# Attention over blocks of 128 keys, one of them shared by two heads, in a fused attention and mixture kernel

## The chip, the cores and the metric

The kernel runs on one NeuronCore of a Trainium2 chip. The metric is the device time of one execution in microseconds (us); the time of a kernel is the median of several executions. The engines are TensorE (PE; its weight loads are listed apart as PEld), VectorE (DVE), ScalarE (ACT), GpSimd (POOL) and SyncE (SP, which here only issues transfers).

## The reference

```python
# 2 batches, 12 heads, 448 rows, head width 64; float32
scores = cap * tanh((q @ k.T / 8) / cap)
attn = exp(scores - rowmax);  attn /= attn.sum(-1) + 1e-9
x = (attn @ v)                      # -> 896 tokens x 768
h = x @ w_in;  x = relu(h)**2 @ w_out          # 768 -> 2048 -> 768, weights float64
e = argmax over 8 experts of cosine(x, emb) / tau
out = gate * relu(x @ w1[e]) @ w2[e]           # 768 -> 1024 -> 768, per token
```

## The kernel before

All matrix work is in float32 of one of two kinds. "f32r" operands go through TensorE in one pass; a product is made exact enough by splitting an operand into a high part (a cast to f32r) and the low rest, and adding two or three products. Plain f32 products go through TensorE as two instructions per matmul, each with a weight load of its own. The array keeps one operand in place (the weights, loaded by LDWEIGHTS) and streams the other one, one column after the other.

The program is written out in order for each engine; each engine takes its own instructions strictly in that order and waits on semaphores. `attention()` is a generator over the 24 heads; the first 13 heads run alone (stage one), and when it yields "batch" the rest is interleaved with the first dense layer, `mlp(0)` (stage two). Then come `mlp(1)`, the routers and the experts, which the change leaves alone but for the order of rows in a chunk of the output.

For each head of the kernel before:

- `load_head` brings q and twice k with rows on 112 partitions (one DMA of q, two of k), `load_v` brings v. A DMA waits until the eighth one before it has landed.
- `split_q` (on POOL) casts q to its high part and subtracts it for the low one. `front_k` (L338) turns k on TensorE, four f32 transposes into PSUM tile `kp`; `front_q` (L352) turns the two parts of q, four f32r transposes into `qp`. VectorE (ScalarE in stage two) casts `kp` to `kh` (L341, L343), VectorE subtracts for the rest `kl` (L345), and `qp` is copied to `q2` (L355, L357).
- `scores` has four blocks of 112 keys, and for each one two f32r matmuls with 448 columns (L371, L372), a tanh by ScalarE (L373) and, for two blocks together, an exp (L374). The result `p_t` stands with keys on partitions.
- `values` multiplies with v: weights are 64 columns of v and 64 of ones, `p_t` is streamed with 448 columns, in plain f32, so 8 passes per head (L384). The ones give the sums of the softmax in 64 rows.
- ScalarE copies the sums into `den` (L393), and `finish` inverts 128x448 of them for two heads (L412) and multiplies (L415); then follow the high part `xh` (L409) and the rest `xl` (L410).

During stage one VectorE also narrows the first dense weights from float64 to float32 (`convert_early`, four operations per chunk, L186 to L189 and L281).

Of the kernel before, what the change touches and what calls it, by code (L numbers as in the profile page):

```python
# [20 lines left out]
def kernel(  # L21
# [22 lines left out]

    nc = tc.nc
# [13 lines left out]
    T = 64  # L59
    OOB = 4096.0  # L60
# [20 lines left out]
    vt = [ap.tile([CP, NC, 2, D], F32, tag=f"vt{i}", name=f"vt{i}", bufs=1) for i in range(2)]  # L81

    def load_head():
        n = nload[0]
        if n >= len(order):
            return
        nload[0] = n + 1
        b, h = order[n]
        q_r = ap.tile([CP, NC, D], F32, tag="q_r", name=f"q_r{n}", bufs=2)
        k_r = ap.tile([CP, NC, 2, D], F32, tag="k_r", name=f"k_r{n}", bufs=2)  # L90
        kk = k[b, h].rearrange("(p c) d -> p c d", c=NC)
        qq = q[b, h].rearrange("(p c) d -> p c d", c=NC)
        e = nc.sync if n else nc.scalar
        if n < 2:
            nc.sync.dma_start(q_r, qq)
        e.dma_start(k_r[:, :, 0, :], kk)
        nc.sync.dma_start(k_r[:, :, 1, :], kk)
        if n >= 2:
            nc.sync.dma_start(q_r, qq)
        raw[n] = (q_r, k_r)  # L100

    def load_v(n):
        b, h = order[n]
        nc.sync.dma_start(vt[n % 2][:, :, h % 2, :], v[b, h].rearrange("(p c) d -> p c d", c=NC))
# [10 lines left out]
    NWARM = 7  # L115
# [4 lines left out]
    def warm(n):  # L120
        for _ in range(n):
            nc.tensor.matmul(idle[:, :S], zero[:, :P], zero, start=True, stop=True)

    warm(NWARM)
    ident = const.tile([P, P], F32, name="ident")
    make_identity(nc, ident)
    identr = const.tile([P, P], F32R, name="identr")
    nc.vector.tensor_copy(identr, ident)
    for i in range(2):
        nc.gpsimd.memset(vt[i][:, :, 1 - i, :], 1.0)  # L130
# [18 lines left out]
    ATN, R1N = 78, 40  # L149
    WC, WM = 4, 3  # L150
    DRIP = 1
    PS, PB = 48, 6
# [116 lines left out]
    def convert_early(step):  # L269

        i, odd = divmod(step, 2)
        if not odd:
            if 0 < i <= len(early):
                c = early[i - 1]
                nc.sync.dma_start(c["keep"](), c["f"])
            if i + 1 < len(early):
                raw_w(early[i + 1], 1001 + i)
        elif i < len(early):
# [3 lines left out]
            for step in narrow(c):  # L282
                step()
# [39 lines left out]
    def attention():  # L323
        pair = {}

        def split_q(n):
            q_r = raw[n][0]
            q_s = ap.tile([CP, NC, 2, D], F32R, tag="q_s", name=f"q_s{n}", bufs=2)
            e = nc.gpsimd if n else nc.vector
            e.tensor_copy(q_s[:, :, 0, :], q_r)  # L330
            e.tensor_tensor(q_s[:, :, 1, :], q_r, f32(q_s[:, :, 0, :]), op=ALU.subtract)
            st[n] = [q_s]

        def front_k(n):
            k_r = raw.pop(n)[1]
            kp = ps.tile([P, S], F32, tag="tr", name=f"kp{n}", bufs=2)
            for c in range(NC):
                nc.tensor.transpose(kp[:, c * CP:(c + 1) * CP], k_r[:, c].rearrange("p t d -> p (t d)"), ident[:CP, :CP])  # L338
            kh = ap.tile([P, S], F32R, tag="kh", name=f"kh{n}", bufs=2)
            if eng["kh"] == "dve" and n:  # L340
                nc.vector.tensor_copy(kh, kp)  # L341
            else:
                nc.scalar.copy(kh, kp)  # L343
            kl = ap.tile([P, S], F32R, tag="kl", name=f"kl{n}", bufs=2)
            nc.vector.tensor_tensor(kl, kp, f32(kh), op=ALU.subtract)  # L345
            st[n] += [kh, kl, []]

        def front_q(n):
            q_s = st[n][0]
            qp = ps.tile([P, S], F32R, tag="tr", name=f"qp{n}", bufs=2)  # L350
            for c in range(NC):
                nc.tensor.transpose(qp[:, c * CP:(c + 1) * CP], q_s[:, c].rearrange("p t d -> p (t d)"), identr[:CP, :CP])  # L352
            q2 = ap.tile([P, S], F32R, tag="q2", name=f"q2{n}", bufs=2)
            if eng["kh"] == "dve":
                nc.vector.tensor_copy(q2, qp)  # L355
            else:
                nc.scalar.copy(q2, qp)  # L357
            st[n][0] = q2

        def front(n):  # L360
            split_q(n)
            load_head()
            front_k(n)

        def scores(n, hf):
            q2, kh, kl, pl = st[n]
            p_t = ap.tile([CP, 2, S], F32, tag="p_t", name=f"p_t{n}_{hf}", bufs=4)
            for j in range(2):
                c = 2 * hf + j
                sc = bank("sc", f"sc{n}_{c}")  # L370
                nc.tensor.matmul(sc[:CP, :S], kh[:, c * CP:(c + 1) * CP], q2, start=True, stop=False)  # L371
# [5 lines left out]
        def values(n):  # L377
# [5 lines left out]
            for c in range(NC):  # L383
                nc.tensor.matmul(pv[:, :S], vv[:, c], pl[c // 2][:, c % 2], start=c == 0, stop=c == NC - 1)  # L384
                if c == 1:
                    yield
# [726 lines left out]
```

## Time and profile before

| | |
|---|---|
| median of 3 runs | 535.78 us (534.64 to 536.04) |
| the profiled execution | 535.34 us, its span from first to last instruction 533.6 us |
| PE busy, granted clock | 98%, 0.995 |
| DVE, ACT, POOL busy | 72%, 58%, 7% |
| stage one, stage two | from about 13 to 82 us, from 82 to about 260 us |

How to read it: busy time is the time in which an engine has at least one instruction in hand. Matmuls overlap in the pipeline, so the duration of one says less than the distance from its start to the next one's start.

### The profile page before, as it was taken

To read this page: it belongs to the slowest core of one execution; us is meant where nothing else is said; L and a number is where in the kernel's file an instruction comes from. 1 tells how busy PE (TensorE), PEld (TensorE's weight loads), DVE (VectorE), ACT (ScalarE), POOL (GpSimd) and SP (SyncE) were. 2 spreads that over 40 slices of the span, in tenths; PEclk is the share of its full clock that TensorE was granted. 3 is DMA by queue.
4 is the path that set the end of the run, shared out by engine and by line. 5 is a ranking of instruction groups with operands and counts; after the bars stand their busy time and mean duration, and the time that the engine had idled before them with its cause. 6 is when DMAs were issued, how large, how long until landed. Compare 5 with 4: busy or idle time off the path is not lost.

```text
span 533.6 us, 7630 instructions
## 1 busy us (share of the span) xinstructions
PE 521.8 (98%) x2558; PEld 439.9 (82%) x2558; DVE 386.7 (72%) x667; ACT 308.3 (58%) x563; POOL 36.4 (7%) x67
## 2 busy tenths in 40 slices
PE   8999999999999999999999999999999999999994
PEld 6676667888888888879999899999889898998993
DVE  4799999999979897989398666645448444556751
ACT  5999899788877878875344331322453233444530
POOL 2221212011011100001000000000000000000000
PEclk9999999999999999999999999999999999999997
DMA  6876994778655858584724213345612245645641
GB/s 145 220 200 154 233 248 136 216 240 270 193 177 184 258 172 249 177 273 155 245 89 135 81 41 118 107 143 155 173 40 80 84 135 170 198 150 153 216 135 38
DMA packets 110713, 87.88 MB, mean 165 GB/s; under 512 B 37442, under 2 KB 97346, under 8 KB 110672
## 3 DMA queue, kind: packets, MB, share of 16 engines
q1 hardware_dynamic: 101904, 81.92, 51.8%
q10 hardware_dynamic: 8672, 5.42, 3.7%
q8 instruction: 21, 0.34, 0.3%
q14 instruction: 20, 0.16, 0.1%
q0 software_dynamic: 96, 0.04, 0.0%
HBM read 69.43 MB, written 18.28 MB: 164 GB/s over the span
## 4 chain that ended last, share of the span: by engine, by line
PE 91%; DVE 4%; ACT 2%; issue 0%; DVEq 0%; ACTq 0%
PE pv L384 11%; PE h L482 7%; PE y L482 7%; PE y L483 7%; PE h L484 7%; PE h L483 7%; PE y L484 7%; PE z L482 4%; PE e L482 4%; PE e L483 4%; PE z L484 4%; PE z L483 4%; PE e L484 4%; PE sc L371 3%; PE sc L372 3%; PE kp L338 1%
## 5 line engine op out<-in xcount | busy, mean ns | idle before, releaser
L215 DVE TENSOR_TENSOR wl<-wf,wh 128x512 fp32r<-128x512 f32 (+1 forms) x140 | 110.3, 799 | 52.5 <-ACT wh L209 50.9
L209 ACT CAST wh<-wf 128x512 fp32r<-128x512 f32 (+1 forms) x97 | 65.8, 697 | 24.4 <-DVE orow L909 8.8
L384 PE MATMUL pv<-p_t,vt 112*128 112x448 f32 x192 | 78.1, 540 | 0.8 <-DVE den L415 0.8
L482 PE MATMUL h<-xh,wh 128*128 128x448 f32 x192 | 76.0, 396 | 0.0
L482 PE MATMUL y<-gh,wh 128*128 128x448 f32 x192 | 75.1, 391 | 0.0
L483 PE MATMUL y<-gh,wl 128*128 128x448 f32 x192 | 70.2, 366 | 0.0
L484 PE MATMUL h<-xl,wh 128*128 128x448 f32 x192 | 70.2, 366 | 0.0
L483 PE MATMUL h<-xh,wl 128*128 128x448 f32 x192 | 70.2, 365 | 0.0
L484 PE MATMUL y<-gl,wh 128*128 128x448 f32 x192 | 70.1, 365 | 0.0
L373 ACT ACTIVATE p_t<-sc,rcap 112x448 f32<-112x448 f32 x96 | 55.4, 629 | 6.6 <-PE sc L372 6.4
L384 PEld LDWEIGHTS pv<-p_t,vt 112*128 112x128 f32 x192 | 36.1, 189 | 25.5 <-issue 22.8
L374 ACT ACTIVATE p_t<-p_t,capb 112x896 f32<-112x896 f32 x48 | 50.1, 1044 | 1.6
L512 ACT ACTIVATE r<-h 128x448 f32<-128x448 f32 x32 | 17.3, 541 | 40.3 <-PE h L484 25.4
L482 PEld LDWEIGHTS h<-xh,wh 128*128 128x128 f32 x192 | 36.1, 188 | 5.2 <-issue 2.4
L483 PEld LDWEIGHTS h<-xh,wl 128*128 128x128 f32 x192 | 36.2, 188 | 4.8 <-issue 2.4
L482 PEld LDWEIGHTS y<-gh,wh 128*128 128x128 f32 x192 | 36.1, 188 | 4.5 <-issue 1.9
L483 PEld LDWEIGHTS y<-gh,wl 128*128 128x128 f32 x192 | 36.2, 188 | 4.3 <-issue 1.9
L484 PEld LDWEIGHTS h<-xl,wh 128*128 128x128 f32 x192 | 36.1, 188 | 3.2 <-DVE xl L410 0.2
L484 PEld LDWEIGHTS y<-gl,wh 128*128 128x128 f32 x192 | 36.1, 188 | 2.9
L371 PE MATMUL sc<-q,kh 128*112 128x448 f32 x96 | 37.3, 389 | 1.1 <-ACT p_t L373 0.9
L211 DVE CAST wh<-wf 128x512 fp32r<-128x512 f32 (+1 forms) x43 | 20.7, 481 | 23.4 <-PE y L484 19.3
L482 PE MATMUL z<-hh,wh 128*128 128x448 f32 x96 | 36.4, 379 | 0.0
(232 smaller groups left out, 942.2 us busy)
## 6 DMA issues: line engine op xcount, KB each, us to landing
wr<-in_moe_w_in_dram SPq DMA_DIRECT2D x16, 768.0 KB, 5.9
wr<-in_moe_w_out_dram SPq DMA_DIRECT2D x24, 512.0 KB, 4.7
wf<-in_moe_w_dram SPq DMA_DIRECT2D x24, 384.0 KB, 3.4
wf<-in_moe_w_dram SPq DMA_DIRECT2D x36, 256.0 KB, 3.2
wf<-wk SPq DMA_DIRECT2D x20, 384.0 KB, 4.0
wk<-wf SPq DMA_DIRECT2D x16, 384.0 KB, 2.8
wk<-wf SPq DMA_DIRECT2D x24, 256.0 KB, 2.7
wf<-wk SPq DMA_DIRECT2D x24, 256.0 KB, 2.9
```

The source lines that it names most:

```text
L209: nc.scalar.copy(c["hi"], c["f"])
L211: nc.vector.tensor_copy(c["hi"], c["f"])
L215: nc.vector.tensor_tensor(c["lo"], c["f"], f32(c["hi"]), op=ALU.subtract)
L371: nc.tensor.matmul(sc[:CP, :S], kh[:, c * CP:(c + 1) * CP], q2, start=True, stop=False)
L372: nc.tensor.matmul(sc[:CP, :S], kl[:, c * CP:(c + 1) * CP], q2, start=False, stop=True)
L373: nc.scalar.activation(p_t[:, j], sc[:CP, :S], AF.Tanh, scale=rcap[:CP])
L374: nc.scalar.activation(p_t, p_t, AF.Exp, scale=capb[:CP])
L384: nc.tensor.matmul(pv[:, :S], vv[:, c], pl[c // 2][:, c % 2], start=c == 0, stop=c == NC - 1)
L482: nc.tensor.matmul(o, wh, xh, start=first, stop=False)
L483: nc.tensor.matmul(o, wl, xh, start=False, stop=False)
L484: nc.tensor.matmul(o, wh, xl, start=False, stop=last)
L512: nc.scalar.activation(r, o[:, :S], AF.Relu)
```

## The change

The two heads of a pair hold 2 x 448 = 896 keys, which are now cut in seven blocks of 128: three of the first head, one in which 64 keys of each head stand, and three of the second. The blocks of all pairs form one stream, taken in groups of two.

- q and k come with 32 x 32 squares on partitions (four DMAs per head, runs of 32 numbers), v as 128-row blocks of 64 columns and one column of ones (two DMAs per head). VectorE turns the squares in one STREAM_TRANSPOSE of 128x448 (`turn`); TensorE turns neither q nor k.
- The keys' high and low parts stand on the two halves of the partitions of one tile `kp`; `qh` holds q's high part twice, `ql` zeros and q's low part. A block's scores are two matmuls as before, four for the shared block, whose keys of the other head are zero columns in `kp`.
- In `split_k` and `split_q` the casts are VectorE's (ScalarE's in stage two), the subtraction for k VectorE's, the second copy and the subtraction for q POOL's. All of them read and write SBUF.
- `values` takes `p_t` as the weights (112 columns at a time) and streams v and the ones: 65 columns, 130 in the shared block. The sums are now a column of the product, so `divide` inverts 112x8 numbers. `finish` turns the rows of a pair back with four f32 transposes on TensorE.
- The products of a pair gather in two PSUM banks. Stage one has two such pairs of banks, stage two one.
- The narrowing of the first weights is handed out one operation per group, and 12 matmuls on zeros stand at the start, where 8 stood.

```diff
-        q_r = ap.tile([CP, NC, D], F32, tag="q_r", name=f"q_r{n}", bufs=2)
-        k_r = ap.tile([CP, NC, 2, D], F32, tag="k_r", name=f"k_r{n}", bufs=2)
+        qk = ap.tile([P, S // SQ, SQ], F32, tag="qk", name=f"qk{n}", bufs=3)
+        for i, a in enumerate((k, q)):
+            halves = a[b, h].rearrange("(s t) (j d) -> j t s d", t=SQ, d=SQ)
+            for j in range(2):
+                e = nc.scalar if n == 0 and j else nc.sync
+                o = (2 * (1 - i) + j) * SQ
+                e.dma_start(qk[o:o + SQ], halves[j])
...
+        def turn(n):
+            qk = raw.pop(n)
+            load_head()
+            tq = ap.tile([P, S], F32, tag="tq", name=f"tq{n}", bufs=2)
+            nc.vector.transpose(tq, qk.rearrange("p s d -> p (s d)"))
+            kp = ap.tile([P, S + D], F32R, tag="kp", name=f"kp{n}", bufs=3)
+            i = n % 2
+            nc.gpsimd.memset(f32(kp[:, :D] if i else kp[:, S:]), 0.0)
+            qh = ap.tile([P, S], F32R, tag="qh", name=f"qh{n}", bufs=3)
...
+        def split_k(n):
+            tq, keys, _, _ = front[n]
+            copy(keys[D:], tq[D:])
+            nc.vector.tensor_tensor(keys[:D], tq[D:], f32(keys[D:]), op=ALU.subtract)
...
+            copy(qh[:D], tq[:D])
+            (nc.gpsimd if n > 1 else nc.vector).tensor_copy(qh[D:], tq[:D])
+            nc.gpsimd.tensor_tensor(ql[D:], tq[:D], f32(qh[:D]), op=ALU.subtract)
...
+        KINDS = [(0, c) for c in range(KB)] + [None] + [(1, c) for c in range(KB)]
...
+                for t, c in parts:
+                    h = st[2 * m + t]
+                    for x in (1, 2):
+                        nc.tensor.matmul(sc[:, :S], h[0][:, c * P:(c + 1) * P], h[x],
...
+                for t in range(NC):
+                    o = acc_[m][t // 2][:, t % 2]
+                    w = p_t[:, j, t * CP:(t + 1) * CP]
...
+                    nc.tensor.matmul(o, w, x, start=i == 0 and t % 2 == 0, stop=i == NK - 1, skip_group_check=True)
+                if i == NK - 1:
+                    divide(m)
+                    if j == 0:
+                        yield from wait(2)
...
+        for g in range(G):
+            if g + 2 < G:
+                scores(g + 2)
                 yield
+                yield from fronts(g + 2)
+            yield from values(g)
```

On PE in stage one, one head of the program before reads as follows. `kp` and `qp` are the turned k and q, `sc` the scores, `pv` the product with v; "x2" counts matmuls, each of which is two passes where operands are plain f32.

```order
L338 MATMUL kp_317<-ident,k_r_203 128x112 x4
L371 MATMUL sc_0_327<-q_285,kh_266 112x448
L372 MATMUL sc_0_327<-q_285,kl_268 112x448
L371 MATMUL sc_1_331<-q_285,kh_266 112x448
L372 MATMUL sc_1_331<-q_285,kl_268 112x448
L352 MATMUL qp_336<-identr,q_s_309 128x112 x4
L371 MATMUL sc_2_344<-q_285,kh_266 112x448
L372 MATMUL sc_2_344<-q_285,kl_268 112x448
L371 MATMUL sc_3_348<-q_285,kh_266 112x448
L372 MATMUL sc_3_348<-q_285,kl_268 112x448
L384 MATMUL pv_361<-p_t_0_270,vt_81 128x448 x2
L384 MATMUL pv_361<-p_t_1_287,vt_81 128x448 x2
```

On PE in the same stage, a group of the changed program and the next one: a shared block (`sc_3`, four matmuls with the keys of two heads), a whole block, and the products of an earlier group; `xp` is a pair's rows turned back.

```order
L400 MATMUL sc_3_314<-qh_206,kp_204 128x448
L400 MATMUL sc_3_314<-ql_121,kp_204 128x448
L400 MATMUL sc_3_314<-qh_241,kp_239 128x448
L400 MATMUL sc_3_314<-ql_119,kp_239 128x448
L400 MATMUL sc_4_320<-qh_241,kp_239 128x448
L400 MATMUL sc_4_320<-ql_119,kp_239 128x448
L421 MATMUL pv_0_244<-vt_82,p_t_254 112x65 x2
L421 MATMUL pv_1_245<-vt_82,p_t_254 112x65 x2
L421 MATMUL pv_0_336<-vt_83,p_t_254 112x65 x2
L421 MATMUL pv_1_337<-vt_83,p_t_254 112x65 x2
...
L458 MATMUL xp_380<-ident,rows_329 128x112 x4
```

The eight transposes of a head are gone, four stand behind every second head, and four matmuls of 448 columns became sixteen matmuls of 65 or 130 columns per group.

On DVE in stage one, what stands for two heads before (`kh`, `kl`, `q` from PSUM, the reciprocal of `den` and two products):

```order
L341 CAST kh_322<-kp_317 128x448
L345 TENSOR_TENSOR kl_324<-kp_317,kh_322 128x448
L355 COPY q_341<-qp_336 128x448
L412 RECIPROCAL den_251<-den_251 128x448
L415 TENSOR_TENSOR den_251<-pv_245,den_251 64x448
L415 TENSOR_TENSOR den_251<-pv_302,den_251 64x448
L341 CAST kh_382<-kp_377 128x448
L345 TENSOR_TENSOR kl_384<-kp_377,kh_382 128x448
L355 COPY q_401<-qp_396 128x448
L410 TENSOR_TENSOR xl_357<-den_251,xh_356 128x448
```

On DVE in the changed program, from the division of a pair to the fifth head's parts; L195 and L197 narrow weights:

```order
L438 TENSOR_SCALAR rs_330<-pv_0_244,ecap 112x4
L438 TENSOR_SCALAR rs_330<-pv_1_245,ecap 112x4
L439 RECIPROCAL rs_330<-rs_330 112x8
L442 TENSOR_TENSOR rows_329<-pv_0_244,rs_330 112x256
L442 TENSOR_TENSOR rows_329<-pv_1_245,rs_330 112x256
L195 SCALAR_TENSOR_TENSOR wf_275<-wr_216,wf_275 128x768
L347 STREAM_TRANSPOSE tq_358<-qk_232 128x448
L380 CAST kp_360<-tq_358 64x448
L359 TENSOR_TENSOR kp_360<-tq_358,kp_360 64x448
L380 CAST qh_362<-tq_358 64x448
L197 SCALAR_TENSOR_TENSOR wf_275<-wr_216,wf_275 128x768
```

The reciprocal shrank from 128x448 to 112x8 numbers, and a head's three operations from PSUM became four from SBUF, of which POOL's copy and subtraction of 64x448 use the results.

## Rows read from the trace of the kernel before

**Rows 1.** The chain of work that ended last, shares of the span by engine.
```profile
PE 91%; DVE 4%; ACT 2%; issue 0%; DVEq 0%; ACTq 0%
```
**Rows 2.** Two windows: us, busy (count) of PE PEld DVE ACT POOL, clock, DMA, GB/s.
```profile
16.00:82.00 66.00, 64.76 (x288) 42.62 (x287) 62.03 (x77) 61.80 (x91) 15.31 (x24) 1.00 0.81 204
82.00:260.00 178.00, 178.00 (x846) 148.38 (x846) 160.28 (x230) 140.08 (x256) 14.46 (x27) 1.00 0.69 212
```
**Rows 3.** Timeline of PE in stage one: start us, us, engine, line, operation, tiles, count.
```profile
66.93 0.45 PE L352 MATMUL qp<-identr,q_s 112*128 112x112 f32 x4
...
67.48 0.36 PE L372 MATMUL sc<-q,kl 128*112 128x448 f32 x1
...
68.08 3.17 PE L384 MATMUL pv<-p_t,vt 112*128 112x448 f32 x8
71.09 0.55 PE L338 MATMUL kp<-ident,k_r 112*128 112x112 f32 x4
...
71.68 0.36 PE L372 MATMUL sc<-q,kl 128*112 128x448 f32 x1
```
**Rows 4.** Timeline of PE's weight loads in stage one.
```profile
66.02 0.18 PEld L371 LDWEIGHTS sc<-q,kh 128*112 128x112 f32 x1
66.12 0.18 PEld L372 LDWEIGHTS sc<-q,kl 128*112 128x112 f32 x1
```
**Rows 5.** Timeline of PE and its loads around a small f32 matmul (cum, two passes).
```profile
406.22 0.32 PE L719 MATMUL cum<-noh,su 112*112 112x64 f32 x2
...
406.32 0.19 PEld L482 LDWEIGHTS e<-x2h,wh 128*128 128x128 f32 x1
...
406.44 0.19 PEld L483 LDWEIGHTS e<-x2h,wl 128*128 128x128 f32 x1
406.64 0.36 PE L483 MATMUL e<-x2h,wl 128*128 128x448 f32 x1
```
**Rows 6.** Groups of instructions in stage one: busy us, mean ns of one, idle before.
```profile
L373 ACT ACTIVATE p_t<-sc,rcap 112x448 f32<-112x448 f32 x48 | 27.7, 627 | 1.4 <-PE sc L372 1.1
L374 ACT ACTIVATE p_t<-p_t,capb 112x896 f32<-112x896 f32 x25 | 26.1, 1043 | 0.8
...
L412 DVE RECIPROCAL den<-den 128x448 f32<-128x448 f32 x6 | 17.6, 2942 | 0.0
...
L345 DVE TENSOR_TENSOR kl<-kp,kh 128x448 fp32r<-128x448 f32 x12 | 7.5, 624 | 0.4
L341 DVE CAST kh<-kp 128x448 fp32r<-128x448 f32 x12 | 7.5, 621 | 4.2 <-PE kp L338 4.0
...
L415 DVE TENSOR_TENSOR den<-pv,den 64x448 f32<-64x448 f32 x10 | 6.2, 622 | 0.3
```
**Rows 7.** Instructions of POOL's lines L330 and L331: ns min/median/max.
```profile
L330 POOL CAST q_s<-q_r x23: 397/398/1202, 5.2 to 180.0; 112x256 fp32r<-112x256 f32 x23
L331 POOL TENSOR_TENSOR q_s<-q_r,q_s x23: 726/737/1328, 5.7 to 180.5; 112x256 fp32r<-112x256 f32 x23
```
**Rows 8.** Instructions of VectorE's cast from SBUF to SBUF.
```profile
L500 DVE CAST gh<-r x32: 383/386/589, 93.4 to 322.2; 128x448 fp32r<-128x448 f32 x32
```
**Rows 9.** Timeline of DVE and POOL where they meet in stage two.
```profile
88.07 0.40 POOL L330 CAST q_s<-q_r 112x256 fp32r<-112x256 f32 x1 [4.81 <-PE qp L352]
...
88.09 0.62 DVE L345 TENSOR_TENSOR kl<-kp,kh 128x448 fp32r<-128x448 f32 x1
...
88.56 0.74 POOL L331 TENSOR_TENSOR q_s<-q_r,q_s 112x256 fp32r<-112x256 f32 x1
88.63 1.48 DVE L215 TENSOR_TENSOR wl<-wf,wh 128x768 fp32r<-128x768 f32 x1
```
**Rows 10.** Timeline of DVE in stage two, two operations in a row.
```profile
112.10 0.62 DVE L410 TENSOR_TENSOR xl<-den,xh 128x448 fp32r<-128x448 f32 x1
112.64 0.38 DVE L500 CAST gh<-r 128x448 fp32r<-128x448 f32 x1
```
**Rows 11.** Timeline of PE at the start, its last wait before the stream.
```profile
12.55 0.46 PE L371 MATMUL sc<-q,kh 128*112 128x448 f32 x1 [0.40 <-ACT p_t L373]
```

More of the change, by code (lines that the diff above doesn't have):

```diff
@@ L267, with convert_early, first @@
     early = []
[L269 to L278, printed above, removed]
+    def convert_early():
+        def first(i):
             c = early[i]
@@ L348, in front_q @@
[L348 to L371, printed above, removed]
-                nc.tensor.matmul(sc[:CP, :S], kl[:, c * CP:(c + 1) * CP], q2, start=False, stop=True)
-                nc.scalar.activation(p_t[:, j], sc[:CP, :S], AF.Tanh, scale=rcap[:CP])
-            nc.scalar.activation(p_t, p_t, AF.Exp, scale=capb[:CP])
-            pl.append(p_t)
@@ L377, in values @@
[L377 to L393 removed]
+        rows = {}
@@ new lines, in divide @@
+        def divide(m):
+            rows[m] = ap.tile([CP, NC, 2, D], F32, tag="rows", name=f"rows{m}", bufs=1)
+            rs = ap.tile([CP, NC, 2], F32, tag="rs", name=f"rs{m}", bufs=2)
+            pv = acc_.pop(m)
+            for t in range(2):
+                nc.vector.tensor_scalar(rs[:, 2 * t:2 * t + 2], pv[t][:, :, :, D], ecap[:CP], None, op0=ALU.add)
+            nc.vector.reciprocal(rs, rs)
+            for t in range(2):
+                c = slice(2 * t, 2 * t + 2)
+                nc.vector.tensor_tensor(rows[m][:, c], pv[t][:, :, :, :D],
+                                        rs[:, c].unsqueeze(3).to_broadcast([CP, 2, 2, D]), op=ALU.mult)
@@ L395, in finish @@
         def finish(m):
             b, h = order[2 * m]
-            den = pair.pop(("d", m))
+            r = rows.pop(m)
             if h == 0:
@@ L422, in attention @@
-        N = len(order)
-        todo = []
-        split_q(0)
-        front_q(0)
-        front_k(0)
-        warm(1)
-        load_head()
+            tp = ps.tile([P, S], F32, tag="tr", name=f"xp{m}", bufs=2)
+            for c in range(NC):
+                nc.tensor.transpose(tp[:, c * CP:(c + 1) * CP], r[:, c].rearrange("p t d -> p (t d)"), ident[:CP, :CP])
+            nc.scalar.copy(xh[:, cc], tp)
+            late.append(lambda: nc.vector.tensor_tensor(xl[:, cc], tp, f32(xh[:, cc]), op=ALU.subtract))
@@ new lines, in fronts, with run_all @@
+        def fronts(g):
+            for m, i in blocks[2 * g:2 * g + 2]:
+                if i in (1, 2, 5, 6):
+                    n = 2 * m + 2 + (i > 4)
+                    if n < N:
+                        if i in (1, 5):
+                            turn(n)
+                            split_k(n)
+                        else:
+                            split_q(n)
+                        yield
+        def run_all(l):
+            while l:
+                l.pop(0)()
+        todo, late, front = [], [], {}
@@ L471, in attention @@
             yield
-        split_pair()
+        run_all(late)
     for n in range(2):
```

208 lines of the change are left out of this document (104 added, 104 removed).

## The prediction

> **What bounds the kernel now.** I read the chain of waits first: 91% of the span lies on TensorE [rows 1]. The windows then tell stage by stage how near the others are. In stage one (16 to 82 us) PE is busy for 64.8 of 66 us, but VectorE for 62.0 and ScalarE for 61.8 as well; in stage two PE is busy throughout, VectorE for 160 of 178 [rows 2]. So a saving on PE counts in full, as long as VectorE and ScalarE give back at least as much. The granted clock is 1.00 in both.
>
> Busy time cannot price a matmul, so I take distances between starts [rows 3]. Three score matmuls from 67.48 to 68.08 make 0.20 us each. The 8 passes of the product with v take 68.08 to 71.09, 3.01, or 0.376 a pass. The four turnings of k begin at 71.09; the second score matmul behind them starts at 71.68, the first one's 0.20 before that, so they take 0.39. In the same way the four of q take 67.28 - 66.93 = 0.35. A pair of heads costs PE 16 x 0.20 + 2 x (3.01 + 0.39 + 0.35) = 10.7 us.
>
> **The change on TensorE.** Removed, for 24 heads: 24 x 3.01 = 72.2 for the products, 9.4 and 8.4 for turning k and q, together 90.0. The scores stay: seven blocks, one of them with four matmuls, are 16 matmuls of 448 columns per pair, as 2 x 8 were. Added: the product takes `p_t` as weights, so each pass has a weight load of 112 columns and streams 65 columns. Per pair there are 6 x 4 x 2 = 48 such passes and 8 with 130 columns, 576 and 96 in all.
>
> What does one cost? Streaming 65 columns is 65/448 of 0.376, or 0.055; 130 columns are 0.11. A load of 112 columns follows the one before it after 0.10 (66.02 to 66.12) [rows 4]. Whether the two overlap is the main question, and one place shows it: cum, f32 in two passes, 112 weight columns, 64 streamed. Its first pass starts at 406.22; the next line's weights begin at 406.32 and the ones after that at 406.44, and L483 starts at 406.64, so the 0.20 of the matmul in front of it began at 406.44 [rows 5]. Two passes and the load of 128 columns that follows take 0.22: about 0.10 for the first pass and 0.11 or 0.12 for the second. That is the loads alone; streaming is hidden under them. I take 0.10 and 0.11: 576 x 0.10 + 96 x 0.11 = 68.2. The turned rows `xp` are four f32 transposes per pair, 12 x 0.39 = 4.7. Added 72.9, removed 90.0: **-17.1 us**. The bounds: 0.055 a pass if only streaming counted (-43), 0.155 if nothing overlapped (+24, a rival below).
>
> A rule speaks against this. The Trainium skill (TensorE: Matmul & The Clock Gate, Part 3, The mechanism) says that LDWEIGHTS overlaps matmuls in flight only when the row group differs, and all these weights span the same rows. By it nothing would overlap; the trace does not agree, since serial passes would have moved the 406.44 start by another 0.05.
>
> **VectorE and POOL in stage one.** A pair costs PE 16 x 0.20 + 48 x 0.10 + 8 x 0.11 + 0.39 = 9.3 us, so both must fit there. Before, VectorE had 62.0/6 = 10.3 per pair [rows 2]. The reciprocal (2.94), two products (1.24) and six operations from PSUM (6 x 0.62) of that go [rows 6]; about 2.4 are left, for `xl` and the narrowing. New per head are the square transpose, two casts and a subtraction. The casts are SBUF to SBUF, 0.39 [rows 8], the subtraction 0.62 as L345. The transpose is in no row: between the cast's 0.39 and the reciprocal's 2.94 for the same 128x448; I take 0.62, the price of everything else that handles one number per lane and step, and keep 2.94 as a rival. That makes 2 x 2.02. `divide` is two products of half the columns (at most 1.24) and three tiny operations; I take 1.5. Together 2.4 + 4.0 + 1.5 = 7.9, less some 0.08 for each of 17 operations, since 112.10 to 112.64 is 0.54 for one listed with 0.62 [rows 10]: about 6.6. ScalarE's seven blocks need 7 x 0.63 + 3.5 x 1.04 = 8.1 and a copy [rows 6]. Both fit under 9.3.
>
> The trouble is where the operands lie. POOL's copy and subtraction grow from 256 to 448 columns: 0.40 to 0.70 and 0.74 to 1.29 if scaled [rows 7], together 1.1 to 2.0 per head. And where POOL meets VectorE the row at 88.63 shows a subtraction of two SBUF operands stretched from 0.95 to 1.48 by a POOL operation of 0.74 begun 0.07 earlier, while L345, with an operand in PSUM, kept its 0.62 beside POOL's cast [rows 9]. Before, q and k were handled from PSUM; now from SBUF. At that rate (0.5 of 0.74) POOL's 4.0 per pair may cost VectorE up to 2.8: 6.6 + 2.8 = 9.4, just at PE's 9.3.
>
> The Trainium skill (SBUF — State Buffer, Who interferes with whom) says the same more strictly: VectorE in a two-port mode or with two SBUF inputs and GpSimd share a port pair, and the later one blocks fully. By it the meeting would cost all 4.0 a pair; the row shows about two thirds.
>
> So what runs late is the chain to q's low part, and it is shortest in slack for the second head of every other pair (blocks 5 and 6 in one group). Count from the start of those scores. PE still does 0.8 for them, then 1.6 of products, 0.39 of `xp`, 0.8 of scores, 1.7 of products and 0.8 of the next scores before it needs it: 6.1. VectorE enters `divide` 0.8 earlier and leaves at 0.7; one narrowing step (0.95) to 1.7, transpose to 2.3, cast, subtraction and cast to 3.7, POOL's subtraction to 5.0, with POOL's copy (0.70) in between 5.7, and one block by a narrowing step (0.5) 6.2. That is even with PE. I charge 0.4 us per pair for the six pairs of stage one, **+2.4**; 0 if it always fits. In stage two PE has dense layers in between, and the casts are ScalarE's; VectorE loses 3 us of work per pair and gains contention, and I charge nothing. The next pair's accumulators there wait for `divide`, with at least 3 us of other matmuls ahead of them (15 of 0.20): covered unless VectorE is 1.5 late, then up to 1 us for each of five pairs.
>
> **The start.** Before, PE streams from 12.55 on [rows 11], with 14 scores and three heads' turnings done (2.8 + 2.2): 7.5 lost. After, VectorE must turn and split three heads one after the other (some 2.2 each with its waits), then POOL subtracts (1.3), before the eighth block; from a first landing near 4 us that is 12.0 to 12.7, with 14 scores, 16 passes and a block (4.8) done: 7.9 lost, **+0.4**, give or take 1.5. The six DMAs per head replace four; each waits for the eighth before it, and two heads' lead (9 us) covers that. The DMA share is 0.81 in stage one [rows 2], so this cover is not large.
>
> **Sum.** Span 533.6 - 17.1 + 2.4 + 0.4 = 519.3; the profiled run had 1.7 around its span, and the median of the runs stands 0.4 above it: 521.4. I say **521.5 us**, 2.7% faster.
>
> **Rivals.**
> - *No stall and cheaper passes.* The chain always fits and a pass is 0.09: another 2.4 + 6 less, 513. For it: 6.6 of 9.3 is not much for VectorE. Against: the load distance of 0.10.
> - *VectorE and POOL take turns in stage one.* If POOL's 4.0 fully add to VectorE's unshortened 7.9, a pair takes 11.9 against 9.3: 6 x 2.6 = 15.6 in place of 2.4, 535, no change. Half of it gives 527. For it: 88.63; against: `divide` and `xl` read PSUM, and POOL can work beside them.
> - *Loads do not hide (slower).* A pass costs 0.10 + 0.055, one of 130 columns 0.21: 576 x 0.155 + 96 x 0.21 = 109.4 in place of 68.2, 563. It decides at a mean of (90.0 - 4.7)/672 = 0.127 per pass. Against it: rows 5, but they are one place with two passes, not a run of 16.
> - *The transpose is slow (slower).* At 2.94, VectorE has 4.6 more per pair: 11.2 before any contention, 12 to 14 with it, so +3 to 5 in each of six pairs, and in stage two 25 more on 160 of 178: 540 to 555.
>
> **How the numbers follow.** Forecast (516 to 527) 0.60; no stall 0.11; half of the port (527 to 534) 0.14; all of it, no change 0.05; loads not hidden 0.04; slow transpose or a starved queue 0.06. No change means within 0.3%, 1.6 us, about what a measurement of this kernel can tell. Faster 0.85, same 0.05, slower 0.10. The range 514 to 531 leaves about 0.2 out.
>
> **What would show it.** A run of 16 product passes in 1.6 us, with loads 0.10 apart; the square transpose near 0.62; VectorE's casts and subtractions stretched where POOL is at work, and score matmuls of the second head of every other pair waiting for POOL's `ql`; stage two starting near 73 instead of 82. Wrong would be passes above 0.127, PE waiting more than 1 us per pair, a lower granted clock in stage one, or PE idle at the division in stage two.

## The result, and the profile after

The changed kernel takes 531.24 us, median of 4 runs (530.42 to 532.13), beside 535.91 for the kernel before: ratio 0.9915, 95% interval 0.989 to 0.9941. It is faster by 4.7 us, where 14 were predicted; 531.24 lies just above the range's 531. Its profiled execution has a span of 529.4 us. Twelve later runs of the same program have a median of 533.93 (ratio 0.9959), so the gain is about 2 to 5 us.

The windows of the changed kernel, stage one from 16 us on, stage two, and the stretch of [rows 2], columns as there:

```profile
16.00:74.00 58.00, 55.47 (x454) 52.95 (x453) 53.80 (x103) 49.99 (x70) 28.15 (x36) 1.00 0.89 207
74.00:241.00 167.00, 158.01 (x950) 145.46 (x949) 141.17 (x235) 119.39 (x218) 19.01 (x26) 1.00 0.71 206
82.00:260.00 178.00, 169.01 (x998) 155.60 (x997) 142.92 (x239) 121.02 (x227) 19.12 (x34) 1.00 0.71 212
```

Stage one ends at 74 us, not 82, as foretold. But from 82 to 260 us, where TensorE was busy for 178.0 of 178 us, it now stands idle for 9.0, although VectorE and ScalarE have less to do there than before (142.9 and 121.0 us).

Multiplying each stretch's matmuls by the distance between their starts gives TensorE's work; what is left of the stretch is idle. Matmuls on zeros at the start do not count as work:

| stretch (ends before / after, us) | work before | after | idle before | after |
|---|---|---|---|---|
| to the first product with v (13.1 / 12.3) | 5.4 | 2.8 | 7.7 | 9.5 |
| to the first dense matmul (82.2 / 73.8) | 67.2 | 56.5 | 1.9 | 5.0 |
| to attention's last work (237.1 / 240.4) | 152.8 | 153.7 | 2.0 | 12.9 |
| to the end (533.6 / 529.4) | 282.8 | 276.6 | 13.8 | 12.3 |

Work fell by 18.6 us; idle rose by 1.9 + 3.1 + 10.9 and fell by 1.5 at the end, 14.4 in all; -18.6 + 14.4 = -4.2, the spans' difference. The entries depend on the distances taken: with the median distance of each kind of matmul in each profile, work falls by 17.4 and idle changes by +2.2, +2.3, +10.9 and -2.3. Either way most of the loss lies in stage two.

TensorE's waits of the changed kernel, first in stage one (13 to 74 us), then in stage two (74 to 241): what waited for what, us in total, times, longest. Stage two of before has no row in this view.

```profile
PE pv L421 <- DMA vs<-in_v_dram: 1.7, 2, 1.4
PE sc L400 <- POOL kp L350: 0.9, 1, 0.9
PE pv L421 <- DMA vt<-in_v_dram: 0.8, 1, 0.8
...
PE pv L421 <- issue: 3.7, 2, 2.5
PE xp L458 <- DVE rows L442: 2.1, 1, 2.1
PE h L525 <- ACT r L555: 1.8, 2, 1.6
PE x2t L568 <- ACT xf L589: 1.3, 2, 0.9
```

"issue" is a name without a cause. The timeline of TensorE and VectorE shows it; TensorE's last dense matmul started at 97.66 us:

```profile
100.57 0.68 PE L421 MATMUL pv<-vt,p_t 128*112 128x65 f32 x5 [2.55 <-issue]
...
97.12 0.95 DVE L223 TENSOR_TENSOR wl<-wf,wh 128x768 fp32r<-128x768 f32 x1
98.00 0.39 DVE L543 CAST gh<-r 128x448 fp32r<-128x448 f32 x1
98.42 0.63 DVE L544 TENSOR_TENSOR gl<-r,gh 128x448 fp32r<-128x448 f32 x1
98.96 0.55 DVE L194 TENSOR_SCALAR wf<-wf 128x768 int32<-128x768 int32 x1
...
100.04 0.75 DVE L442 TENSOR_TENSOR rows<-pv,rs 112x256 f32<-112x256 f32 x2
```

The product is the next pair's first one. It starts when VectorE has read the old pair's first bank out of PSUM (the first of the two operations of L442), and that read stands behind work on weights and on the dense layer. From 91.87 us on VectorE works without a pause, and GpSimd meets it there once:

```profile
92.37 1.47 POOL L366 TENSOR_TENSOR ql<-tq,qh 64x448 fp32r<-64x448 f32 x1 [2.66 <-PE sc L400]
...
92.81 1.28 DVE L543 CAST gh<-r 128x448 fp32r<-128x448 f32 x1
```

That cast takes 0.39 when alone (98.00 above), so in this row GpSimd accounts directly for 0.9 of the 2.55 us; from 94.2 us to the pause's end it does nothing. A second chain ends at ScalarE; its waits in stage two, and the rows around 136 us:

```profile
ACT kp L382 <- DVE tq L347: 21.3, 8, 5.8
...
135.52 0.96 DVE L197 SCALAR_TENSOR_TENSOR wf<-wr,wf 128x768 int32<-128x768 int32 x1
136.40 0.64 DVE L347 STREAM_TRANSPOSE tq<-qk 128x448 f32<-128x448 f32 x1
...
137.07 0.56 ACT L382 CAST kp<-tq 64x448 fp32r<-64x448 f32 x1 [5.85 <-DVE tq L347]
137.65 0.55 ACT L555 ACTIVATE r<-h 128x448 f32<-128x448 f32 x1
```

ScalarE reached k's cast 5.85 us before the transpose that it needs. The relu L555 stood behind the cast, and TensorE behind the relu (1.8 us). Before, this cast waited for TensorE's own turning, 2.3 us in three times.

### The profile page after: what moved, and what is told of

It reads as the page before. It is cut to its first block, busy times and chain, and to the rows that moved or that the text cites. A ratio compares the mean times of both kernels' runs of the same rounds, so it can differ in the third digit from the quotient of the medians.

```text
span 529.4 us, 8393 instructions
## 1 busy us (share of the span) xinstructions
PE 507.0 (96%) x2898; PEld 461.8 (87%) x2898; DVE 372.7 (70%) x715; ACT 282.2 (53%) x521; POOL 58.1 (11%) x100
## 4 chain that ended last, share of the span: by engine, by line
PE 70%; DVE 12%; DMA 6%; issue 5%; ACT 3%; SPq 2%; POOL 0%; ACTq 0%; DVEq 0%; POOLq 0%
PE y L525 6%; PE y L526 6%; PE y L527 6%; PE pv L421 6%; PE h L525 5%; PE h L527 5%; PE h L526 5%; PE z L525 4%; PE e L525 4%; PE e L526 4%; PE e L527 4%; PE z L527 4%; PE z L526 4%; PE sc L400 4%; DVE wl L223 3%
## 5 line engine op out<-in xcount | busy, mean ns | idle before, releaser
L223 DVE TENSOR_TENSOR wl<-wf,wh 128x512 fp32r<-128x512 f32 (+1 forms) x140 | 112.4, 814 | 63.4 <-ACT wh L217 58.7
L525 PE MATMUL h<-xh,wh 128*128 128x448 f32 x192 | 72.0, 375 | 1.8 <-ACT r L555 1.8
L525 PE MATMUL y<-gh,wh 128*128 128x448 f32 x192 | 72.3, 376 | 0.0
L421 PEld LDWEIGHTS pv<-vt,p_t 128*112 128x112 f32 x576 | 62.8, 178 | 7.4 <-issue 4.8
L421 PE MATMUL pv<-vt,p_t 128*112 128x65 f32 x576 | 62.3, 259 | 4.5 <-issue 3.7
L402 ACT ACTIVATE p_t<-sc,rcap 128x448 f32<-128x448 f32 x84 | 49.0, 630 | 16.9 <-PE sc L400 16.9
L403 ACT ACTIVATE p_t<-p_t,capb 128x896 f32<-128x896 f32 x42 | 43.9, 1044 | 1.4
L400 PE MATMUL sc<-qh,kp 128*128 128x448 f32 x96 | 37.4, 389 | 3.0 <-DVE kp L359 1.8
L366 POOL TENSOR_TENSOR ql<-tq,qh 64x448 fp32r<-64x448 f32 x23 | 30.8, 1339 | 61.0 <-ACT qh L382 33.1
L555 ACT ACTIVATE r<-h 128x448 f32<-128x448 f32 x32 | 17.2, 538 | 37.8 <-PE h L527 25.7
```

Source lines behind the costliest of these rows:

```text
L223: nc.vector.tensor_tensor(c["lo"], c["f"], f32(c["hi"]), op=ALU.subtract)
L366: nc.gpsimd.tensor_tensor(ql[D:], tq[:D], f32(qh[:D]), op=ALU.subtract)
L400: nc.tensor.matmul(sc[:, :S], h[0][:, c * P:(c + 1) * P], h[x], start=t == parts[0][0] and x == 1, stop=t == parts[-1][0] and x == 2)
L402: nc.scalar.activation(p_t[:, j], sc[:, :S], AF.Tanh, scale=rcap)
L403: nc.scalar.activation(p_t, p_t, AF.Exp, scale=capb)
L421: nc.tensor.matmul(o, w, x, start=i == 0 and t % 2 == 0, stop=i == NK - 1, skip_group_check=True)
```

## The experiments

All times are medians of 4 to 12 runs, each beside runs of the kernel before (535.5 to 536.0 us).

| kernel | us | ratio to before (95%) |
|---|---|---|
| changed kernel again | 533.93 | 0.9959 (0.9938 to 0.998) |
| wait4 | 528.53 | 0.9848 (0.9824 to 0.9872) |
| late_k | 530.60 | 0.9913 (0.9885 to 0.9941) |
| wait4_late_k | 525.47 | 0.9802 (0.9783 to 0.9821) |
| pool_out | 530.59 | 0.9903 (0.9881 to 0.9926) |
| v_early | 535.35 | 0.9983 (0.9968 to 0.9998) |
| v_early_fill | 535.60 | 0.9999 (0.9981 to 1.0017) |
| wr_actq | 547.61 | 1.0217 (1.0194 to 1.0241) |
| wlk_v4 | 524.58 | 0.9812 (0.9781 to 0.9842) |
| wlk_qk_long | 523.02 | 0.9778 (0.9755 to 0.9801) |
| wlk_ps44 | 531.62 | 0.9937 (0.9906 to 0.9968) |
| wlk_ps56 | 530.80 | 0.9910 (0.9894 to 0.9926) |
| wlk_v4_pool | 527.60 | 0.9841 (0.9817 to 0.9865) |
| wlk_v4_start | 525.08 | 0.9807 (0.9785 to 0.983) |
| wlk_v4_split2 | 524.95 | 0.9785 (0.9759 to 0.9811) |
| wlk_v4_split2_wait | 523.35 | 0.9764 (0.9748 to 0.9779) |

My theory was the order: VectorE and ScalarE take their rows in turn, and what TensorE needs stands too far back. The rival was the port that VectorE shares with GpSimd.

**wait4**: the next pair's first product comes later.

```diff
-    ATN, R1N = 76, 40
+    ATN, R1N = 82, 40
...
-                        yield from wait(2)
+                        yield from wait(4 if eng["kh"] == "act" else 2)
```

`ATN`, the number of attention's steps that are spread over the dense layer, rises by the six steps that the waits add (three pairs, two each), in this kernel and in all with its edit; the diffs below leave it out.

> In stage two, where a pair ends in the first half of a group (three of the six pairs there), 30 matmuls of the dense layer stand between its last product with v and the next pair's first one, where the changed kernel has 15; nothing else is changed. Theory one (order: the next pair's products wait for the division, which stands behind a backlog in VectorE's row): the pauses of TensorE at 97.9 us (2.7) and 161.2 us (1.3) go, 4.0 us in all, 527.5 us (526.5 to 528.5). Theory two (VectorE is made slow by GpSimd at the shared port): the backlog itself is what is paid, a later product only moves the pause to the next place that needs VectorE or ScalarE, and at least half comes back: 529.5 to 531.5 us.

**late_k**: k's cast and subtraction are issued with q's in stage two.

```diff
-                            split_k(n)
+                            if eng["kh"] != "act":
+                                split_k(n)
                         else:
+                            if eng["kh"] == "act":
+                                split_k(n)
                             split_q(n)
```

> In stage two the cast and the subtraction for k are issued together with those for q, a few dense matmuls behind the square transpose, where they stood right behind it. Theory one (ScalarE takes its row in order and stands at the cast of k until VectorE reaches the transpose, 21.3 us in 8 waits, with the relu, the squares and the copies behind it): the pauses of TensorE at 136.4 us (1.8, for the relu's output), 184.5 (0.5) and 199.7 us (1.1, for a copy) go, 3.4 us, 528 us (527 to 529.5). Theory two (VectorE itself is late because of GpSimd): the cast comes later, but so does everything on VectorE that the dense layer needs, 530.5 to 532 us.

**pool_out**: no GpSimd in stage two's split of q.

```diff
+            if eng["kh"] == "act":
+                nc.vector.tensor_copy(qh[D:], tq[:D])
+                return
             (nc.gpsimd if n > 1 else nc.vector).tensor_copy(qh[D:], tq[:D])
```

> In stage two GpSimd's cast and subtraction for q are taken away: the second copy of q's high part is made by VectorE, and the low part of q is left out of the scores of those heads (they use what stood in the buffer). VectorE gets ten casts of 0.39 us more (3.9) and loses its stretches, some 0.9 us for each of ten heads. Theory one (order): a division still stands behind the same operations in VectorE's row and ScalarE's casts still wait for the transposes, so most of TensorE's 12.9 us of idle time in stage two stays: 9 or more, 527 to 530 us. Theory two (the port): with GpSimd gone the idle time in stage two falls below 4 us: 521 to 524 us.

TensorE's waits from 78 to 241 us, in the order wait4, late_k, pool_out:

```profile
PE h L525 <- ACT r L555: 1.6, 1, 1.6
PE pv L421 <- issue: 0.6, 1, 0.6
PE x2t L568 <- ACT xf L589: 0.3, 1, 0.3
```
```profile
PE xp L458 <- DVE rows L442: 2.1, 1, 2.1
PE pv L421 <- issue: 1.0, 2, 0.6
PE sc L400 <- ACT p_t L402: 0.3, 1, 0.3
```
```profile
PE xp L461 <- DVE rows L445: 2.1, 1, 2.1
PE pv L424 <- issue: 1.5, 2, 0.9
PE h L528 <- ACT r L558: 1.1, 1, 1.1
PE x2t L571 <- ACT xf L592: 0.5, 1, 0.5
```

wait4 cut the wait for the division from 3.7 to 0.6 us, took the last pair's 2.1 away as well, and left the relu's 1.6. late_k took the relu's and the copy's, 3.1 us, and also 2.7 of the 3.7 before the next pair's products: the two chains are linked. With GpSimd gone, 5.2 of 8.9 us stay, although VectorE then has ten casts more: the port lengthens these waits by some 3.7 us, the order makes the larger part. wait4 came out 1 us above the time foretold, late_k 2.6, and pool_out 0.6 above its range. By its time alone late_k would lie in its rival's range (530.5 to 532); it is the waits that speak for the order. Stage one, which they share with the changed kernel, was longer than in its first profile (next run but one).

**wait4_late_k**: both edits.

> Both edits of stage two together: 30 dense matmuls ahead of the next pair's first product where a pair ends in the first half of a group, and k's cast issued with q's. Alone, the first left pauses of TensorE at 134 (0.7), 139 (1.8, ScalarE's relu) and 201 us (0.5), the second at 103 (0.6), 220 (0.7) and 238 us (2.3). If they are two mechanisms, both kinds go, stage two has under 2 us in pauses of over 0.25, and the time is 525 to 527.5 us. If VectorE has no room left (rival), a new pause of 1 to 3 us comes, 528 to 530 us.

525.47 us, as the theory said: in stage two TensorE's only listed wait is one of 0.5 us. From the changed kernel run again (533.93) wait4 gains 5.4 us, late_k 3.3 and both 8.5, so the gains nearly add, though the chains are linked.

**The changed kernel again** (after_again).

> The changed kernel itself once more, beside the others. In four kernels that share its stage one (all but one of them word for word) stage one had 7.7 to 9.6 us of idle time on TensorE, where the first profile of the changed kernel has 5.0, and the granted clock fell to half at about 72 to 80 us, behind a pause of 2.1 to 3.1 us. If stage one is the same program with a time that varies (theory: transfers that land late, and a clock that falls after a long pause), this run has 7 to 10 us there, a clock below 1.00 at 72 to 80, and 532 to 535 us. If those kernels' edits did it, it has 5 us and 531.2 us.

533.93 us, runs from 530.77 (mean clock 0.997) to 536.89 (0.985): stage one varies by itself, as the theory said. Windows of this run:

```profile
12.00:20.00 8.00, 8.00 (x42) 7.65 (x41) 7.29 (x14) 5.95 (x9) 4.81 (x7) 0.57 0.96 251
...
72.00:76.00 4.00, 1.75 (x13) 1.37 (x13) 3.90 (x9) 3.27 (x5) 1.54 (x2) 1.00 0.84 113
76.00:80.00 4.00, 4.00 (x22) 3.74 (x22) 3.21 (x6) 2.25 (x4) 0.71 (x1) 0.63 1.21 294
```

From 12 to 20 us the granted clock was 0.57 of the full 2.4 GHz, so for most of the stretch TensorE ran at its lower level, 1.2 GHz: 42 matmuls where the first profile has 60; it had stood idle for 1.9 us from 9.3 on. Another fall to 0.63 follows the pause for `vt` at 73 us. The kernel before has no pause over 0.8 us after 16 us; its granted clock in [rows 2] is 1.00.

**v_early, v_early_fill**: the second head's v earlier; then also zeros in the pause at 9 us.

```diff
-                if i == 5 and 2 * m + 3 < N:
+                if i == 3 and 2 * m + 3 < N:
```
```diff
+                    if g == t == 1:
+                        for _ in range(8):
+                            nc.tensor.matmul(idle[:, :S], zero[:, :P], zero, start=True, stop=True)
```

> The transfer of v of a pair's second head is issued two blocks earlier (behind the third block's products of the pair before, where it stood behind the sixth's). Theory (transfers): TensorE's pauses of 1.6 us at 45.3 us and 0.4 at 35.1 us, in which products of the shared block wait for the small part of v, go: 2.0 us, 529.2 us (528.5 to 530). Rival (VectorE and GpSimd bound stage one): the next wait for q's or k's low part takes their place, 531 us; or the queue of transfers is full, the part lands no earlier, and the pause stays, 531 us.

> The kernel with the early transfer of v (535.4 us; in its profile the granted clock was 0.50 to 0.68 from 12.4 to 20 us, behind a pause of 2.05 us at 9 us), with eight matmuls on zeros in that pause. Theory (the pause makes the clock fall): the clock stays 1.00 from 12 to 20 us and 3 to 4 us are won: 531 to 532.5 us. Rival (the clock falls for another reason, or the zeros' matmuls delay the scores): within 1 us of 535.4.

The waits for v's small part at 35 and 45 us went (0.2 us left; 0.9 with the zeros), but the one at the end of stage one grew to 2.8, and with the zeros, which did hold the clock at 1.00 from 12 to 20 us, to 4.8. What stage one wins it gives back at 70 us, in a wait for a transfer. Both times stayed at the upper end of what the changed kernel's runs show, so both expectations of a gain fell.

**wr_actq**: the raw weights on ScalarE's queue.

```diff
-        nc.sync.dma_start(c["raw"], c["src"]())
+        (nc.scalar if eng["kh"] == "dve" else nc.sync).dma_start(c["raw"], c["src"]())
```

> In stage one the loads of raw weights (768 KB each) are issued on ScalarE's queue, the loads of q, k and v stay on SyncE's. Theory (one queue: what is issued behind such a load lands 5 to 7 us later, not 2.3, and products with v wait for it): v lands in 2.5 to 3.5 us, TensorE's pauses at 35, 45 and 71 us, 3 to 5.5 us together, go, and with them the fall of the clock behind the last one; 4 to 6 us less than the changed kernel beside it. Rival (the transfer engines are full, whichever queue feeds them; their share is 0.88 in stage one): v lands as late as before and the time is within 1 us. Rival (ScalarE bound): ScalarE issues eight loads of some 0.5 us and is itself at 7.1 of 8, scores wait for its tanh: 0 to 4 us slower.

Transfers of this kernel from 26.7 us on, on SyncE and on ScalarE, and SyncE's wait:

```profile
26.71 1.05 SPq L104 DMA_DIRECT2D qk<-in_k_dram  x2
27.80 5.85 SPq L104 DMA_DIRECT2D qk<-in_q_dram  x2
...
28.45 0.38 ACTq L185 DMA_DIRECT2D wr<-in_moe_w_in_dram  x1
...
SPq L104 <- DMA wr<-in_moe_w_in_dram: 5.0, 1, 5.0
```

13.7 us slower than the changed kernel beside it, where the slowest theory had 4. The program gives its transfers eight semaphores in turn, so a transfer waits until the eighth one before it in the program's order has landed, and this holds across both queues: SyncE's second issue of the pair at 27.80 waited 5.0 us for the weights, which ScalarE had issued late, at 28.45. v did land sooner, in a median of 2.5 us in place of 3.7, as the theory had it; what a second queue would bring without that wait the run does not show.

**wlk_qk_long, wlk_ps44, wlk_ps56, wlk_v4**, all on wait4_late_k: long packets for q and k (the scores are then those of other rows, so the result is not that of the kernel); the first weights' loads earlier (44) or later (56); a fourth buffer for v. The last diff is cut to the loads.

```diff
-            halves = a[b, h].rearrange("(s t) (j d) -> j t s d", t=SQ, d=SQ)
+            halves = a[b, h].rearrange("(j t s) (u d) -> j t (s u) d", j=2, t=SQ, d=SQ)
```
```diff
-    PS, PB = 50, 6
+    PS, PB = 44, 6
```
```diff
-                if i == 1 and 2 * m + 2 < N and m:
-                    load_v(2 * m + 2)
-                if i == 5 and 2 * m + 3 < N:
+                if i == 1 and 2 * m + 3 < N:
                     load_v(2 * m + 3)
+                if i == 5 and 2 * m + 4 < N:
+                    load_v(2 * m + 4)
```

> On the same kernel: q and k come with the same bytes in the same DMAs, but in runs of 448 numbers (1792 bytes), where the changed kernel reads 32 (128 bytes), so that the scores are those of rows and columns of q and k in another order. Theory (the short packets of the new layout fill the transfer engines): the share of the transfers in stage one falls from 0.87 to below 0.80, v lands earlier, stage one's pauses of some 4 us and the fall of the clock behind the last go: 520 to 522 us. Rival (a packet's length doesn't matter here, the raw weights do): the share stays above 0.84 and the time within 1 us of 525.5.

> On the same kernel: the loads of stage two's first weights begin six steps (some 4 us) earlier in stage one. If the end of stage one is bound by the sum of its transfers, spreading them helps: v's pause at 71 us shrinks by 1 to 2 us, 523 to 524.5 us. If only the order in the queue counts, the same loads stand before another v, and a pause of the same size appears a pair earlier: 525 to 526 us.

> On the same kernel: the loads of stage two's first weights begin six steps (some 4 us) later. If they are what delays v at the end of stage one, the pause at 71 us and the fall of the clock go and stage one ends 3 to 4 us earlier; the first dense matmuls then wait for weights by 0 to 3 us: 522 to 525 us. If not, the pause stays and the wait for weights is added: 526 to 529 us.

> On the kernel with both edits of stage two (525.5 us): a fourth buffer for v, and each v issued about half a pair (some 4.7 us) earlier. Theory (v is late because it stands in the one queue behind 768 KB of raw weights): the pauses of TensorE at 36 (0.3), 46 (1.4) and 71 us (2.3), and the fall of the clock behind the last, go: 3.5 to 5 us, 520.5 to 522 us. Rival (the transfers of stage one as a whole bound its end; their share is above 1.0 from 60 to 72 us): the pause at 71 us stays or moves to q or k, stage one still ends at 76 to 77 us: 524.5 to 526 us.

Packets and the queue's share of 16 engines' time, from 13 to 73 us, of wait4_late_k, then of wlk_qk_long:

```profile
DMA packets 32272, 11.50 MB, mean 192 GB/s; under 512 B 26747, under 2 KB 31355, under 8 KB 32264
...
q1 hardware_dynamic: 32264, 11.40, 87.3%
```
```profile
DMA packets 13945, 12.46 MB, mean 208 GB/s; under 512 B 6214, under 2 KB 12913, under 8 KB 13937
...
q1 hardware_dynamic: 13937, 12.36, 74.7%
```

The same loads in long packets: 75% of the engines' time in place of 87, for more bytes. So the short packets cost transfer time. In the kernel's time it is 2.5 us by the medians and 1.3 by the ratios (0.9802 and 0.9778, whose intervals overlap), less than the 3.5 to 5.5 expected; TensorE still waits 2.0 us for v. Moving the weights' loads failed either way, with times above every range given. Six steps earlier they stood ahead of more of the v's (TensorE's waits for v 7.0 us in place of 3.5); six steps later stage one ended at 73.2 us, but the dense layer then paused 3.0 us at 96 and the next division 2.4 at 132. With v early its waits are gone, and others stand there; the time, 524.58, lies in the rival's range. TensorE's waits from 13 to 82 us of wlk_v4, and VectorE's row ahead of the second one:

```profile
PE xp L459 <- DVE rows L443: 2.5, 2, 2.0
...
68.91 0.55 DVE L220 CAST wh<-wf 128x768 fp32r<-128x768 f32 x1
69.49 1.78 DVE L224 TENSOR_TENSOR wl<-wf,wh 128x768 fp32r<-128x768 f32 x1
...
71.81 0.76 DVE L443 TENSOR_TENSOR rows<-pv,rs 112x256 f32<-112x256 f32 x2
```

It is the division again, behind a weight's subtraction that GpSimd stretched from 0.95 to 1.78 us.

**wlk_v4_pool, wlk_v4_start, wlk_v4_split2, wlk_v4_split2_wait**, on wlk_v4: GpSimd's split of q taken away from the fourth head on (the edit of pool_out under `if n > 2`); two edits at the start, of which the first diff shows one (the other puts five matmuls on zeros into TensorE's pause); one weight chunk less split ahead; and that with a wait behind each pair (`ATN` 86).

```diff
-            nc.gpsimd.tensor_tensor(ql[D:], tq[:D], f32(qh[:D]), op=ALU.subtract)
+            (nc.gpsimd if n > 1 else nc.vector).tensor_tensor(ql[D:], tq[:D], f32(qh[:D]), op=ALU.subtract)
```
```diff
-    AHEAD = {"load": 6 + NRAW, "conv0": 6, "conv1": 5, "store": 4, "split": 3}
+    AHEAD = {"load": 6 + NRAW, "conv0": 6, "conv1": 5, "store": 4, "split": 2}
```
```diff
-                    if j == 0:
+                    if eng["kh"] == "act":
+                        yield from wait(2 if j else 4)
+                    elif j == 0:
                         yield from wait(2)
```

> On the kernel with both edits of stage two and the early v (524.6 us): GpSimd's cast and subtraction for q are taken away from the fourth head on; VectorE makes the second copy of q's high part, and the low part of q is left out of those heads' scores (they use what stood in the buffer). In stage one TensorE waits there for the division at 51 (0.7) and 70 us (2.1), in VectorE's row behind operations that GpSimd stretched (0.95 to 1.78 us). Theory (the port is what is left of stage one's loss on VectorE): both pauses go, stage one ends 2 to 3 us earlier, 521 to 522.5 us. Rival (VectorE's row itself is full; the ablation adds 0.39 us per head): the pauses stay within 0.5 us, 524 to 526 us. Rival (the transfers are next): the pause becomes one for v or q of 1 to 2 us, 523 to 524.5 us.

> On the same kernel (524.6 us), two edits at the start: the second head's subtraction for q is VectorE's, where GpSimd's stretched VectorE's cast from 0.39 to 1.23 us, and five matmuls on zeros stand in TensorE's pause of 2.05 us at 8.4 us. Theory: the second head's scores come 0.5 to 1 us earlier, the clock does not fall behind the pause, and stage one carries it to its end: 523 to 524 us, and the mean clock of the runs rises from 0.993 to 0.995 or more. Rival (stage one's end is set by transfers and VectorE, not by its start): within 0.5 us of 524.6.

> On the kernel with both edits of stage two and the early v (524.6 us): a weight chunk is split into its two parts two chunks ahead of its use, where three were. In VectorE's row one cast and one subtraction of 128x768 (0.55 and 1.78 us, stretched by GpSimd) move from ahead of the division that ends stage one to behind it. Theory (order on VectorE: that division is late by what stands ahead of it): the pause of 2.1 us at 70 us goes, and the time is 522 to 523 us. Rival (the pause comes back as a wait for the weights at the first dense matmuls, or for v's transfer): 524 to 526 us.

> The same, and where a pair ends in the second half of a group in stage two, some more dense matmuls before the next pair's first product, as in the first half. Theory: the pause of 2.6 us that the kernel with the early v has at 128 us (its division stands behind four operations on weights) goes as well: 520 to 521.5 us. Rival (attention then ends later than the dense layer needs it, or the rate of steps brings another wait): 522 to 525 us.

Without GpSimd the subtraction takes 0.96 and the pauses for the division 0.45 and 1.24 us in place of 0.66 and 2.13: the port is some 1.1 us of them, the rest stays with VectorE's row, which has a cast more per head. The time rose nevertheless, to 527.6, above every range given. Its profile has a clock of 0.62 from 12 to 20 us, but the clock is not all: a run with a mean of 0.997 took 527.12, and the two of wlk_v4 at 0.997 took 523.44 and 523.50. Why it is slower stays open; the added casts are a candidate that was not tested. wlk_v4_start brought nothing (525.08), as the rival said; its stage one ended at 72.9 us, that of wlk_v4 at 72.8. Moving the order halved the pause at 70 us (2.13 to 0.98), and stage one ended at 71.0; alone it left the pause of 2.6 us at 127 and the time (524.95). With the wait that pause went too, and others of 1.5 us at 96 and 1.8 at 188 came: 523.35 us, 0.9764 of before, in the rival's range (522 to 525), not the theory's, and the lowest median with the whole computation; its interval overlaps that of wlk_v4_split2, so the last step alone is not told from noise. Its TensorE waits from 13 to 82 us have one row left:

```profile
PE xp L461 <- DVE rows L445: 0.9, 1, 0.9
```

## Why the prediction was wrong

- **TensorE's work** (-17.1 predicted): right, -18.6 (-17.4 with median distances). One timeline row shows a group's 16 passes, from 205.75 to 207.34 us, 1.59, as foretold:

```profile
205.75 0.91 PE L421 MATMUL pv<-vt,p_t 128*112 128x65 f32 x8
206.49 1.09 PE L421 MATMUL pv<-vs,p_t 128*112 128x130 f32 x8
207.34 0.45 PE L525 MATMUL y<-gh,wh 128*128 128x448 f32 x1
```

- **VectorE's and GpSimd's prices**: right. The transpose takes 0.64 (0.62 taken), GpSimd's copy and subtraction have medians of 0.71 and 1.23 (0.70 and 1.29). Summary of their lines:

```profile
L347 DVE STREAM_TRANSPOSE tq<-qk x24: 628/636/645, 4.6 to 198.9; 128x448 f32<-128x448 f32 x24
L365 POOL CAST qh<-tq x22: 552/708/918, 11.7 to 199.7; 64x448 fp32r<-64x448 f32 x22
L366 POOL TENSOR_TENSOR ql<-tq,qh x23: 1132/1228/1792, 8.7 to 209.7; 64x448 fp32r<-64x448 f32 x23
```

- **The port**: under-priced. I took 0.5 us of stretch for 0.74 of GpSimd's. A cast of 0.39 that met a subtraction of 1.26 begun 0.28 earlier took 1.23 and ended 0.25 behind it:

```profile
8.73 1.26 POOL L366 TENSOR_TENSOR ql<-tq,qh 64x448 fp32r<-64x448 f32 x1 [4.73 <-DVE qh L380]
...
9.01 1.23 DVE L380 CAST kp<-tq 64x448 fp32r<-64x448 f32 x1
```

  The Trainium skill (SBUF — State Buffer, Who interferes with whom) has the later one blocked fully; by that rule the cast would have ended 0.39 behind the subtraction, not 0.25, so the trace nearly agrees. It did not decide the time: pool_out shows that the larger part of stage two's waits stands without it.
- **Stage one's stall** (+2.4): +3.1 (+2.3 with median distances), the size right by chance, the cause wrong. I had q's low part late; no wait of TensorE is for it. 2.5 us are v's. The 0.9 listed as GpSimd's came otherwise: its operation (L350) was over at 14.71, and the score matmul began at 15.38, when ScalarE's first tanh had ended (14.66 to 15.28). ScalarE had stood for a minimum of one column, which took VectorE 1.13 us beside GpSimd's subtraction (13.37 to 14.50):

```profile
13.38 1.13 DVE L150 TENSOR_TENSOR ecap<-ecap,capb 128x1 f32<-128x1 f32 x1
...
14.55 0.20 ACT L151 ACTIVATE ecap<-ecap 128x1 f32<-128x1 f32 x1 [1.12 <-DVE ecap L150]
14.66 1.14 ACT L402 ACTIVATE p_t<-sc,rcap 128x448 f32<-128x448 f32 x2
```

  My step that two heads' lead covers the six DMAs asked only for q and k. v is issued half a pair ahead, behind 768 KB of weights, among packets that are now short; and in the profiles where it made TensorE pause for 2 us and more the clock fell as well.
- **The start** (+0.4, give or take 1.5): +1.9, mis-sized. TensorE stood for 1.8 us from 9.2 us on for the second head's k, whose cast is the stretched one above.
- **Stage two**: this is the step that failed, "I charge nothing". Idle time there rose by 10.9 us, more than the 9.7 by which the forecast missed. I had seen that the next pair's products wait for the division with 15 matmuls ahead of them and called it covered unless VectorE was 1.5 us late, then up to 1 us a pair, which I left out of the sum. VectorE was later than that: TensorE paused for 2.5 and 1.2 us before the products of the two worst pairs. I had named PE idle at the division as a sign of being wrong, and it came. I had not asked whether a lower total on VectorE makes it punctual. It doesn't: its row is a mix of weights, dense layer and attention, and a tensor's place in it counts. That ScalarE stands at k's cast until VectorE reaches the transpose I had not seen at all. wait4_late_k, which moves only these two places, is 8.5 us below the changed kernel run again (533.93 to 525.47); 7.8 of it is idle time in stage two (12.0 to 4.2, counted as in the table above).
- **The end** (-1.5) belongs to neither: from the last transfer's issue to the span's end it is 5.7 us in the profile before and 4.1 in the one after, and 6.0 in wlk_v4_start.
- The rivals: serial loads and a slow transpose fell. VectorE and GpSimd taking turns gave the nearest numbers (527 to 535), but in stage one, where most of the loss was not.

What stays open: why the clock falls behind the pause at 9 us in some runs and not in others of the same program; why wlk_v4_pool is slower than wlk_v4; and how much of 523.35 is still the short packets, which no layout tried here avoids with the result intact.

## What to carry to other kernels

When work moves from the bounding engine to one with room, do not ask only whether its busy time fits: look up in each in-order row what stands ahead of the new operation, and who waits behind it on every other engine. Put slack where a value is handed over (a later consumer, a cast issued when its input is surely there); two such edits of a few lines were worth more (8.5 us) than the change itself (2 to 5). After freeing an engine, expect the next bound in the same stage (here v's transfers, then the division), and move one at a time.

## What the hardware did that was not expected

- Behind a pause of TensorE of some 2 us or more the granted clock fell in part of the profiles (0.57 from 12 to 20 us and 0.63 from 76 to 80 us in after_again) and not in others: in the first profile of the same program it stayed 1.00 behind the pause of 2.55 us. Twelve runs of that program spread over 6 us.
- VectorE's operations that read PSUM (L438, L442, L460) and its 32x32 transpose kept their time beside GpSimd's subtraction (the transpose in the two places where they met); others, from SBUF to SBUF, grew by up to 1.0 us each.
- The program's limit of eight transfers in flight is shared by the queues of two engines: one late issue on ScalarE stopped SyncE for 5.0 us.
